# Exact two-valued one-hot rows in a clustered attention with experts: no counts, no masks of q, the row of maxima in the first product

## The chip, the cores and the metric

The program runs on one core of a Trainium2 chip. The metric is device time in microseconds (us) of one execution. The kernel before has a median of 580.08 us over 3 runs (579.9 to 581.32). A profiler recorded one more execution; it took 577.12 us, and the span from its first to its last instruction is 575.0 us.

## The reference

There are 4 batches, 8 heads, 768 positions, head size 64, 16 centroids per head. Each query and each key belongs to the cluster of its nearest centroid (largest cosine). A query attends only to the keys of its own cluster; where its cluster has no keys, every score is equal, and it takes the mean of all values.

```python
mask = q_assign[:, :, :, None] == k_assign[:, :, None, :]
scores = scale * np.matmul(q, k.transpose(0, 1, 3, 2))
scores = np.where(mask, scores, -1000000000.0)
scores = scores - np.max(scores, axis=-1, keepdims=True)
attn = np.exp(scores)
attn = attn / (np.sum(attn, axis=-1, keepdims=True) + 1e-09)
return np.matmul(attn, v).astype(np.float32)
```

The result is 3072 tokens of 512 numbers. A gate picks one of 8 experts for each token, every expert keeps the 80 tokens of highest gate weight, and gives `gate * (max(x @ w1, 0) @ w2)` (1024 hidden units); all other tokens give zero.

## The kernel before

Heads are worked in 16 pairs. Each of q and k is split into a high part (rounded to the short f32 format of one PE pass) and the rest. `KAB` and `QAB` are the six buffers of two planes each: plane 1 holds high and low parts (rows 0 to 63 low k against high q, rows 64 to 127 high k against low q), plane 0 holds the high parts in rows 0 to 63, the one-hot rows of the cluster in rows 64 to 79 and one row more, 80. A score tile is the sum of two products (`scores`, L478 over 128 rows of plane 1, L479 over 81 rows of plane 0); the maxima (`smax`, L441 on PE and L443 on VectorE) take rows 0 to 79 of plane 0. The one-hot row of k is 0 where the key is in the cluster and -1 elsewhere, that of q is 2^100 in its cluster and 0 elsewhere, so that a product over other clusters falls to -2^100. Row 80 is -1 in k, and in q the row of maxima (`shift`), which is so subtracted inside the product. ScalarE then takes the exponential (L484), GpSimd sums the probabilities (L493), PE multiplies with the values (`av`, L502, four matmuls in a group, 96 groups).

`assign` finds the clusters of a pair: similarities (L213), a transpose (L221), equality with the maximum on VectorE (L225, L227), transposes back (L231), a product that resolves ties (L237). For queries whose cluster has no keys it counts: the largest value of each row (L243), a flag (L244), a one-column product (L246) that brings the flag to the rows of q, a factor (L249), and the one-hot rows of q times that factor (L251). A product of these rows with a constant (L300) gives a mask, and VectorE multiplies q with it (L302), so that such a query has q = 0 and no one-hot row, and all its scores are 0. `pair` splits and copies the tensors (L268, L273, L282, L307, copies at L82); `first` and `beside` do the same for the first pair.

The order of all this is not written out. Each part yields steps with an engine, an assumed duration, needs and a due time; a planner (`Flow`) plays the steps through with these numbers and writes the instructions to each engine's queue in the order that results. The due times and some holds are in the table `CFG`. Where PE would be idle at the start, it adds products of ones (L1459). Queues run in order; SP issues nearly all copies. Behind the attention come the gate, the choice of 80 tokens for each expert (a chain of small steps), and the experts, whose weights are converted on ScalarE and VectorE.

Of the kernel before, what the change touches and what calls it, by code (L numbers as in the profile page):

```python
# [7 lines left out]
F32 = mybir.dt.float32  # L8
F32R = mybir.dt.float32r
# [10 lines left out]
CFG = dict(at=dict(sum=-3.87, av=6.53, xT=13.56, lt=4.68, turn=2.79, sm=0.38, exp=-3.44, mx=-2.09), stick=0.98,  # L20
           wait=0.04, idle=0.25, dummy=128, bias=0.22, side=(-1.31, -0.22), prep=(-0.75, 0.12), lead=(-39.19, -31.86,
           -37.55, -36.75, -19.29), zero=(-15.19, 0.47, -13.33, 0.15), start=dict(pe=6.1, act=4.8, dve=7.5, pool=2.5,
           dma=0.0), warm=48, cold=38.0, lag=1.3, hold=dict(dve=(0.2, -0.02), act=(0.42, 0.05), pe=(0.26, -0.02)),
           nab=6, pps=9, sums=8, xts=4, vs=2, skew=3, raws=4, lds=3, keys=1, adds=7, weigh=(8, 5.0, 1.5), slots=(19,
           5), native1=(), native2=(0, 1, 2, 4), early=((2, 6), 185.8), spread=(), mix=dict(ld=-44.02, st=-11.35,
           hi1=3.94, lo1=-19.15, hi2=-1.45, lo2=12.52, xg=-48.58, xp=-11.37, out=18.87, sc=3.79, a0=16, a1=14, a2=10,
           spare=-0.17, half=15, reserve=10, eager=10))
# [14 lines left out]
class Program:  # L42
# [41 lines left out]
    def setup(self):  # L84
# [12 lines left out]
        self.twos, self.id4096 = (K16[:, i * P + NT:(i + 1) * P + NT] for i in (3, 4))  # L97
        self.digit = [K16[0:E, 5 * P + NT + i * E:5 * P + NT + (i + 1) * E] for i in range(4)]
# [5 lines left out]
        self.ident, self.hsel = view["ident"], view["hsel"]  # L104
# [6 lines left out]
        self.sel = con.tile([P, NP, P], F32R, name="sel")  # L111
# [91 lines left out]
    def assign(self, b, p):  # L203
# [32 lines left out]
        fi = self.misc([P, 512])  # L236
        nc.tensor.matmul(fi[:, 0:HS], lhsT=self.tie, rhs=es, start=True, stop=True)  # L237
        yield Step("act", .58, also=("dve", .95), needs=[("ohq", *divmod(r - 2, self.NP))] if r > 2 else [])
        oh = st["oh", b, p] = w.tile([P, HS], F32R, name="oh", bufs=2)
        nc.scalar.activation(oh[0:64], fi[0:64, 0:HS], AF.Identity, bias=self.negone[0:64])  # L240
        z = w.tile([P, 1], F32, name="z", bufs=2)
        z16 = w.tile([P, 1], F16, name="zh", bufs=2)
        nc.vector.tensor_reduce(z[0:64], fi[0:64, 0:HS], axis=AX.X, op=ALU.max)  # L243
        nc.vector.tensor_scalar(z16[0:64], z[0:64], 0.5, None, op0=ALU.is_gt)  # L244
        yield Step("pe", .1)
        nc.tensor.matmul(fi[:, HS:HS + 1], lhsT=self.twos[0:64], rhs=z16[0:64], start=True, stop=True)  # L246
        yield Step("dve", .15)
        ne = w.tile([P, 1], F32, name="ne", bufs=2)
        nc.vector.tensor_scalar(ne, fi[:, HS:HS + 1], 0.5, BIG, op0=ALU.is_gt, op1=ALU.mult)  # L249
        yield Step("act", .58, give="misc", key=("oh", b, p))  # L250
        nc.scalar.activation(oh[64:P], fi[64:P, 0:HS], AF.Relu, scale=ne[64:P])  # L251

    def pair(self, b, p):
# [32 lines left out]
        yield Step("none", 0.0, key=("full", "k", b, p), dma=[CP] * 2)  # L286
        for i, g in enumerate(pos):
            copy(self.KAB[g][0:D, 1, :], lo[i * D:(i + 1) * D, :])
        yield Step("none", 0.0, needs=[("oh", b, p)], key=("hi", "k", b, p), late=CFG["lag"], dma=[OH] * 4)
        onehot("k", self.KAB)  # L290
        yield Step("none", 0.0, needs=[("ld", "q", b, p), ("oh", b, p)], key=("ohq", b, p), late=CFG["lag"], dma=[OH] * 4)
        onehot("q", self.QAB)
# [15 lines left out]
        yield Step("none", 0.0, key=("full", "q", b, p), dma=[CP] * 4)  # L308
        for i, g in enumerate(pos):
            copy(self.QAB[g][0:D, 1, :], hi[i * D:(i + 1) * D, :])  # L310
# [9 lines left out]
    def first(self):  # L320
# [37 lines left out]
        fk, cnt, fq = one([P, HS], "st1"), one([P, 1], "st2"), self.spare([P, HS])  # L358
# [25 lines left out]
        for f in range(2):  # L384
            nc.tensor.matmul(mask[f], lhsT=self.sel[:, 2 + f, :], rhs=oh, start=True, stop=True)
# [1388 lines left out]
```

## Time and profile before

| | us |
|---|---|
| median of 3 runs | 580.08 (579.9 to 581.32) |
| profiled execution | 577.12 |
| its span | 575.0 |
| PE busy in the span | 550.9 |
| VectorE busy | 436.6 |
| GpSimd busy | 377.9 |
| ScalarE busy | 375.4 |

The page gives the busy time of each engine and the granted clock of PE over 40 slices. The views used below are the table of windows (busy time in a stretch), the timeline (instructions in order of time), the lines (instructions grouped by line of the kernel) and the waits. PE is the matmul engine, PEld its weight loads, DVE VectorE, ACT ScalarE, POOL GpSimd, SPq the queue of SyncE. An f32 matmul of the values is recorded twice.

### The profile page before, as it was taken

The page shows a single profiled execution, that of the slowest core. Times are in us where ns is not written, and L with a number is a line of the kernel's source. Part 1 is how long each engine was busy: PE and PEld are TensorE (multiplying, and loading weights), DVE is VectorE, ACT ScalarE, POOL GpSimd, SP SyncE. Part 2 cuts the span into 40 slices and gives each one's busy share as a digit, 9 for nine tenths or more (in the row PEclk, how much of TensorE's full clock was granted, in tenths as well). Part 3 has the DMA queues.
Part 4 walks back from the last instruction along what each step waited for, and adds up shares of the span by engine and source line. Part 5 has one row for each costly group of instructions (what it writes and reads, how often), then busy time and mean ns, then how long its engine had stood idle before and what let it go on. Part 6 is the DMA issues. An engine that isn't in the chain of part 4 may idle for free. (4 is left out here: it accounts for less than half of the span.)

```text
span 575.0 us, 11207 instructions
## 1 busy us (share of the span) xinstructions
PE 550.9 (96%) x3939; PEld 358.6 (62%) x3939; DVE 436.6 (76%) x867; ACT 375.4 (65%) x743; POOL 377.9 (66%) x225
## 2 busy tenths in 40 slices
PE   7899999999999999999999999999999977999996
PEld 6566666566657675656566565666765455766574
DVE  4977677777768787767777786797869467997983
ACT  7747777686748676866676775758655363755661
POOL 6339795977597796939796969397995021434531
PEclk9869999999999999999999999999999978999999
DMA  7385667768566858677559577445655595599931
GB/s 256 86 236 152 177 187 205 182 185 233 131 184 179 245 166 221 177 216 172 151 156 239 160 220 188 113 122 133 202 212 219 200 338 184 172 308 387 388 122 34
DMA packets 69591, 112.67 MB, mean 196 GB/s; under 512 B 11328, under 2 KB 38496, under 8 KB 69536
## 3 DMA queue, kind: packets, MB, share of 16 engines
q1 hardware_dynamic: 68512, 109.32, 65.1%
q0 software_dynamic: 1024, 2.64, 1.5%
q8 instruction: 31, 0.51, 0.4%
q14 instruction: 24, 0.20, 0.1%
HBM read 70.96 MB, written 13.99 MB: 148 GB/s over the span
## 5 line engine op out<-in xcount | busy, mean ns | idle before, releaser
L443 DVE TENSOR_REDUCE mx<-sm 128x1 f32<-128x384 f32 x384 | 202.6, 551 | 50.9 <-PE sm L441 49.0
L493 POOL TENSOR_TENSOR sum<-sum,pp 128x768 f32<-128x768 f32 x121 | 217.7, 1832 | 3.2 <-ACT pp L484 2.8
L484 ACT ACTIVATE pp<-st 128x384 f32<-128x384 f32 x384 | 173.4, 486 | 65.4 <-PE st L479 57.0
L502 PE MATMUL av<-pp,ldv 128*64 128x384 f32 x768 | 144.2, 498 | 0.0
L441 PE MATMUL sm<-KAB,QAB 80*128 80x384 f32 x384 | 139.4, 381 | 1.4 <-DVE mx L443 0.6
L478 PE MATMUL st<-QAB,KAB 128*128 128x384 f32 x384 | 135.7, 353 | 0.0
L479 PE MATMUL st<-QAB,KAB 81*128 81x384 f32 x384 | 130.3, 339 | 0.0
L441 PEld LDWEIGHTS sm<-KAB,QAB 80*128 80x128 f32 x384 | 71.3, 192 | 31.8 <-DVE mx L443 12.0
L493 POOL TENSOR_TENSOR sum<-pp 128x768 f32<-128x768 f32 x32 | 58.4, 1830 | 49.5 <-ACT pp L484 49.5
L502 PEld LDWEIGHTS av<-pp,ldv 128*64 128x64 f32 x768 | 46.9, 136 | 62.8 <-issue 60.5
L478 PEld LDWEIGHTS st<-QAB,KAB 128*128 128x128 f32 x384 | 73.4, 191 | 9.1 <-issue 4.8
L479 PEld LDWEIGHTS st<-QAB,KAB 81*128 81x128 f32 x384 | 73.5, 191 | 0.0
L307 POOL TENSOR_TENSOR ldq<-ldq,hi 128x768 fp32r<-128x768 f32 x15 | 27.3, 1818 | 32.5 <-ACT hi L268 30.2
L972 POOL DMA_INDIRECT xg<-xs,gi x8 | 22.0, 2751 | 38.8 <-PE tp L989 19.0
L1376 DVE TENSOR_REDUCE most<-weigh 128x1 f32<-128x1024 f32 x32 | 38.7, 1209 | 4.7 <-DMA weigh<-in_w_dram 4.7
L282 POOL TENSOR_TENSOR ldk<-ldk,hi 128x768 fp32r<-128x768 f32 x15 | 27.3, 1821 | 7.9 <-issue 7.8
L948 DVE SCALAR_TENSOR_TENSOR w1p<-raw,scales,w1p 128x512 f16<-128x512 f32 (+1 forms) x36 | 29.3, 862 | 2.5 <-ACT w1p L939 2.5
L1022 PEld LDWEIGHTS <-w1p 128*128 128x128 f16 x768 | 28.6, 100 | 3.8 <-issue 3.8
L1022 PE MATMUL hp<-xt,w1p 128*128 128x80 f16 x768 | 29.5, 202 | 0.3 <-DVE xt L1000 0.3
L1081 POOL DMA_INDIRECT out_dram<-room,si x8 | 11.6, 1445 | 26.3 <-ACT room L1074 16.1
L939 ACT ACTIVATE w1p<-raw,scales 128x1024 f16<-128x1024 f32 x22 | 24.0, 1141 | 2.1 <-DMA raw<-in_w_dram 2.1
L273 ACT CAST QAB<-hi 64x768 fp32r<-64x768 f32 x30 | 25.0, 832 | 0.7
(253 smaller groups left out, 687.9 us busy)
## 6 DMA issues: line engine op xcount, KB each, us to landing
raw<-in_w_dram SPq DMA_DIRECT2D x34, 512.0 KB
weigh<-in_w_dram SPq DMA_DIRECT2D x32, 512.0 KB
room<-in_w_dram SPq DMA_DIRECT2D x25, 512.0 KB
ldk<-in_kT_dram SPq DMA_DIRECT2D x16, 384.0 KB
ldq<-in_qT_dram SPq DMA_DIRECT2D x16, 384.0 KB
ldv<-in_v_dram SPq DMA_DIRECT2D x16, 384.0 KB
out_dram<-zero SPq DMA_DIRECT2D x24, 256.0 KB
QAB<-hi SPq DMA_DIRECT2D x31, 192.0 KB
```

The lines of the kernel that those rows point to most:

```text
L282: nc.gpsimd.tensor_tensor(lo, t, hi.bitcast(F32), op=ALU.subtract)
L307: nc.gpsimd.tensor_tensor(lo, t, hi.bitcast(F32), op=ALU.subtract)
L441: nc.tensor.matmul(s, lhsT=qj, rhs=k[0:D + C, 0, f * HS:(f + 1) * HS], start=True, stop=True)
L443: nc.vector.tensor_reduce(mx[:, j, f:f + 1], s, axis=AX.X, op=ALU.max)
L478: nc.tensor.matmul(s, lhsT=k[:, 1, ks], rhs=q[:, 1, qs], start=True, stop=False)
L479: nc.tensor.matmul(s, lhsT=k[0:D + C + 1, 0, ks], rhs=q[0:D + C + 1, 0, qs], start=False, stop=True)
L484: self.nc.scalar.activation(self.st["pp", g, c][:, f], self.st.pop(("s", g, c, f)), AF.Exp, scale=float(self.D) ** -0.5)
L493: eng.tensor_tensor(flat(t), flat(a), flat(self.st["pp", g, c]), op=ALU.add)
L502: nc.tensor.matmul(a[i * D:(i + 1) * D, f, 0:HS], lhsT=v[:, c, i, :], rhs=st["pp", 2 * r + i, c][:, f], start=(c == 0), stop=(c == NC - 1) ...
L948: nc.vector.scalar_tensor_tensor(t[:, 1, fs], raw[:, 0, fs], s, t[:, 0, fs], op0=ALU.mult, op1=ALU.subtract)
L1022: nc.tensor.matmul(hp[:, f, :], lhsT=wt[:, a, fs], rhs=xt[:, x, k, :], start=(k == 0 and i == 0), stop=(k == K - 1 and i == 2))
L1376: nc.vector.tensor_reduce(self.most[:, R + n:R + n + 1], t, axis=AX.X, op=ALU.max, apply_absolute_value=True)
```

## The change

The one-hot rows become exact: `hit` makes 2^100 or 0 for q, `miss` makes 0 or -1 for k. For a query of an empty cluster every score is now q.k - 2^100, which rounds to -2^100, and so does its maximum; the difference is 0 if the maximum is added before -2^100 is. So the row of maxima moves to the first product: it takes row 0 of plane 1, and the row that was there moves to row 80 of plane 0. The counts (L243 to L249), the mask products (L300) and the products of q (L302) are gone. Copies of 64 rows into plane 1 become one of 63 rows and one of a single row. The one-hot rows of k and q are copied in one step of their own (`ohs`). The table `CFG` has new due times, and two steps of `shift` are bound to follow each other.

```diff
-CFG = dict(at=dict(sum=-3.87, av=6.53, xT=13.56, lt=4.68, ...
+CFG = dict(at=dict(sum=-1.08, av=6.7, xT=10.95, lt=4.66, ...
...
-        oh = st["oh", b, p] = w.tile([P, HS], F32R, name="oh", bufs=2)
-        nc.scalar.activation(oh[0:64], fi[0:64, 0:HS], AF.Identity, bias=self.negone[0:64])
-        nc.vector.tensor_reduce(z[0:64], fi[0:64, 0:HS], axis=AX.X, op=ALU.max)
-        nc.vector.tensor_scalar(z16[0:64], z[0:64], 0.5, None, op0=ALU.is_gt)
-        nc.tensor.matmul(fi[:, HS:HS + 1], lhsT=self.twos[0:64], rhs=z16[0:64], start=True, stop=True)
-        nc.vector.tensor_scalar(ne, fi[:, HS:HS + 1], 0.5, BIG, op0=ALU.is_gt, op1=ALU.mult)
-        nc.scalar.activation(oh[64:P], fi[64:P, 0:HS], AF.Relu, scale=ne[64:P])
+        st["oh", b, p] = w.tile([P, HS], F32R, name="oh", bufs=2)
+        self.rows(st["oh", b, p], fi, fi)
+        yield Step("none", 0.0, needs=self.vacated(g0), key=("ohs", b, p), late=CFG["lag"], dma=[OH] * 8)
+        for n, AB in (("k", self.KAB), ("q", self.QAB)):
+            for i in range(2):
+                self.onehot(AB[(g0 + i) % CFG["nab"]], st["oh", b, p], n == "q", i)
+    def hit(self, dst, src):
+        self.nc.scalar.activation(dst, src, AF.Relu, scale=BIG)
+    def miss(self, dst, src):
+        self.nc.vector.tensor_scalar(dst, src, 1.0, -1.0, op0=ALU.is_ge, op1=ALU.add)
+    def rows(self, oh, fk, fq):
+        self.hit(oh[64:P], fq[64:P])
+        self.miss(oh[0:64], fk[0:64])
...
+        def split(AB, src):
+            for i, g in enumerate(pos):
+                copy(AB[g][1:D, 1, :], src[i * D + 1:(i + 1) * D, :])
+                copy(AB[g][D + C:D + C + 1, 0, :], src[i * D:i * D + 1, :])
...
-            nc.tensor.matmul(mask, lhsT=self.sel[:, 2 + f, :], rhs=self.st["oh", b, p], start=True, stop=True)
-            nc.vector.scalar_tensor_tensor(t[:, fs], mask, 1.0 / BIG, t[:, fs], op0=ALU.mult, op1=ALU.mult)
...
-        for i, g in enumerate(pos):
-            copy(self.QAB[g][0:D, 1, :], hi[i * D:(i + 1) * D, :])
+        split(self.QAB, hi)
...
+        def const(AB, key):
+            return [*moved(AB), (Step("pool", .7, key=key), lambda: nc.gpsimd.memset(AB.bitcast(F32)[0:1, 1, :], -1.0))]
...
-        self.copy(q[D + C:D + C + 1, 0, :].rearrange("o (j p) -> o j p", p=P), row)
+        self.copy(q[0:1, 1, :].rearrange("o (j p) -> o j p", p=P), row)
...
-            nc.gpsimd.memset(t.bitcast(F32)[64:96, 0, :], -1.0)
+            nc.gpsimd.memset(t.bitcast(F32)[0:1, 1, :], -1.0)
```

PE's queue while the fourth pair is prepared, before (`sm` maxima, `st` scores, `av` values, `zh` the flags of the count, `sel` the constant of the mask; the numbers behind names are buffers):

```order
L441 MATMUL sm<-KAB_114,QAB_108 128x384
L502 MATMUL av<-pp,ldv 64x384 x4
L300 MATMUL misc<-oh,sel 128x384
L441 MATMUL sm<-KAB_114,QAB_108 128x384 x2
L478 MATMUL st<-QAB_106,KAB_112 128x384
L479 MATMUL st<-QAB_106,KAB_112 128x384
L478 MATMUL st<-QAB_106,KAB_112 128x384
L479 MATMUL st<-QAB_106,KAB_112 128x384
L300 MATMUL misc<-oh,sel 128x384
L478 MATMUL st<-QAB_107,KAB_113 128x384
L479 MATMUL st<-QAB_107,KAB_113 128x384
```

The same place of the program after the change, where the ties product (L236, before L237) is the last product of the assignment (the lines of the scores are now L459 and L460, of the maxima L428):

```order
L460 MATMUL st<-QAB_105,KAB_111 128x384
L236 LDWEIGHTS K_62
L236 MATMUL misc<-es,K_62 128x384
L428 MATMUL sm<-KAB_113,QAB_107 128x384
L459 MATMUL st<-QAB_106,KAB_112 128x384
L460 MATMUL st<-QAB_106,KAB_112 128x384
L428 MATMUL sm<-KAB_113,QAB_107 128x384
L459 MATMUL st<-QAB_106,KAB_112 128x384
L460 MATMUL st<-QAB_106,KAB_112 128x384
L483 MATMUL av<-pp,ldv 64x384 x4
```

The two mask products that stood among scores have no successor, nor has the count ten rows above them.

VectorE's queue at the start, from the one-hot rows of the first head to the second head's maxima, before (`z`, `zh`, `ne` belong to the counts, `mx` are the maxima, `mr` those over all keys):

```order
L243 TENSOR_REDUCE z<-misc 64x1
L244 TENSOR_SCALAR zh<-z 64x1
L388 SCALAR_TENSOR_TENSOR ldq<-st,ldq 128x384 x2
L411 CAST QAB_104<-ldq 64x768
L443 TENSOR_REDUCE mx<-sm 128x1 x4
L249 TENSOR_SCALAR ne<-misc 128x1
L443 TENSOR_REDUCE mx<-sm 128x1 x3
L302 SCALAR_TENSOR_TENSOR ldq<-misc,ldq 128x384
L443 TENSOR_REDUCE mx<-sm 128x1
L302 SCALAR_TENSOR_TENSOR ldq<-misc,ldq 128x384
L457 TENSOR_TENSOR m_472<-mx 128x6
L458 SCALAR_TENSOR_TENSOR mr<-m_472 128x6
```

After (`amx` and `eq` find the clusters, L254 makes the rows of k):

```order
L254 TENSOR_SCALAR KAB_109<-st 16x384 x2
L224 TENSOR_REDUCE amx<-misc 128x24
L226 TENSOR_TENSOR eq<-misc,amx 128x384
L254 TENSOR_SCALAR oh_327<-st 64x384
L430 TENSOR_REDUCE mx<-sm 128x1 x6
L254 TENSOR_SCALAR oh<-misc 64x384
L430 TENSOR_REDUCE mx<-sm 128x1 x6
L439 TENSOR_REDUCE mr<-mx 128x6
L430 TENSOR_REDUCE mx<-sm 128x1 x12
L439 TENSOR_REDUCE mr<-mx 128x6
```

The counts and the four products of q are gone from between the maxima; two one-hot halves are new.

SP's queue with the copies of the third pair, before (`hi` high parts, `ldk` the rest of k, `oh` one-hot rows, `row` the row of maxima):

```order
L82 DMA KAB_114<-ldk 64x768
L82 DMA KAB_115<-ldk 64x768
L82 DMA KAB_114<-oh 16x384 x2
L82 DMA KAB_115<-oh 16x384 x2
L82 DMA QAB_108<-oh 16x384 x2
L82 DMA QAB_109<-oh 16x384 x2
L195 DMA ldk<-in_kT_dram 128x768
L82 DMA QAB_106<-row 1x6x128
```

After:

```order
L82 DMA KAB_113<-oh 16x384 x2
L82 DMA KAB_114<-oh 16x384 x2
L82 DMA QAB_107<-oh 16x384 x2
L82 DMA QAB_108<-oh 16x384 x2
L82 DMA QAB_105<-row 1x6x128
L82 DMA KAB_113<-ldk 63x768
L82 DMA KAB_113<-ldk 1x16x48
L82 DMA KAB_114<-ldk 63x768
L82 DMA KAB_114<-ldk 1x16x48
```

The row of maxima of an earlier head stands among these copies, and each copy of the rest of k is now two.

## Rows read from the trace of the kernel before

**Rows 1.** The page: busy us, share, instructions; clock in tenths over 40 slices.
```profile
PE 550.9 (96%) x3939; PEld 358.6 (62%) x3939; DVE 436.6 (76%) x867; ACT 375.4 (65%) x743; POOL 377.9 (66%) x225
...
PEclk9869999999999999999999999999999978999999
```

**Rows 2.** Windows of the span; columns are named in the first row.
```profile
core 0: us, PE busy (x) PEld busy (x) DVE busy (x) ACT busy (x) POOL busy (x), PEclk, DMA share, GB/s
44.00:450.00 406.00, 401.49 (x2347) 257.69 (x2347) 310.54 (x617) 278.82 (x593) 319.33 (x178) 1.00 0.66 181
450.00:488.00 38.00, 29.62 (x385) 20.85 (x384) 23.46 (x80) 17.99 (x29) 5.92 (x12) 0.87 0.84 269
488.00:565.00 77.00, 75.79 (x952) 51.02 (x953) 69.43 (x85) 47.95 (x64) 29.73 (x12) 1.00 0.74 261
```

**Rows 3.** Timeline of PE: a mask product inside a run (start, duration).
```profile
122.80 0.34 PE L479 MATMUL st<-QAB,KAB 81*128 81x384 f32 x1
122.98 0.34 PE L300 MATMUL misc<-oh,sel 128*128 128x384 f32 x1
123.16 0.33 PE L478 MATMUL st<-QAB,KAB 128*128 128x384 f32 x1
```

**Rows 4.** Lines of PE from 44 to 450 us: busy us, mean ns.
```profile
L300 PE MATMUL misc<-oh,sel 128*128 128x384 f32 x27 | 10.0, 371 | 0.0
...
L246 PE MATMUL misc<-zh,K 64*128 64x1 f16 x13 | 2.1, 163 | 1.6 <-DVE zh L244 1.5
```

**Rows 5.** Timeline of PE: a count inside a run.
```profile
116.20 0.33 PE L441 MATMUL sm<-KAB,QAB 80*128 80x384 f32 x1
116.69 0.16 PE L246 MATMUL misc<-zh,K 64*128 64x1 f16 x1 [0.16 <-DVE zh L244]
116.78 0.44 PE L478 MATMUL st<-QAB,KAB 128*128 128x384 f32 x1
117.06 0.34 PE L479 MATMUL st<-QAB,KAB 81*128 81x384 f32 x1
```

**Rows 6.** Timeline: value groups, alone and two in one run.
```profile
100.75 0.62 PE L441 MATMUL sm<-KAB,QAB 80*128 80x384 f32 x2
101.30 1.51 PE L502 MATMUL av<-pp,ldv 128*64 128x384 f32 x8
102.74 0.55 PE L527 MATMUL misc<-K,xT 128*128 128x128 f32 x3
...
450.78 2.80 PE L502 MATMUL av<-pp,ldv 128*64 128x384 f32 x16
...
453.51 2.79 PE L544 MATMUL sm<-sum,unit 128*32 128x384 f32 x32
```

**Rows 7.** Waits of PE and its loads, 44 to 450 us: us, times, longest.
```profile
PE misc L221 <- ACT row L464: 2.0, 9, 0.3
...
PEld sm L441 <- DVE mx L443: 7.0, 12, 0.7
```

**Rows 8.** The start: timeline of ScalarE, VectorE and PE.
```profile
9.47 1.44 ACT L400 CAST KAB<-ldk 64x384 fp32r<-64x384 f32 x3
...
15.48 0.54 DVE L443 TENSOR_REDUCE mx<-sm 128x1 f32<-128x384 f32 x1
...
30.03 1.16 PE L441 MATMUL sm<-KAB,QAB 80*128 80x384 f32 x2
31.37 1.15 PE L441 MATMUL sm<-KAB,QAB 80*128 80x384 f32 x2
32.09 1.02 DVE L443 TENSOR_REDUCE mx<-sm 128x1 f32<-128x384 f32 x2 [0.31 <-PE sm L441]
32.32 0.52 PE L478 MATMUL st<-QAB,KAB 128*128 128x384 f32 x1
```

**Rows 9.** Copies of L82 on SP: ns min/median/max to issue; who waited.
```profile
L82 SPq DMA_DIRECT2D QAB<-oh x64: 507/587/1315, 18.6 to 399.9; - x64
...
L82 SPq DMA_DIRECT2D QAB<-row x32: 694/762/838, 28.0 to 431.2; - x32
...
  PEld av L502: 0.6, 1
```

**Rows 10.** Lines of GpSimd from 44 to 450 us.
```profile
L493 POOL TENSOR_TENSOR sum<-sum,pp 128x768 f32<-128x768 f32 x120 | 215.9, 1832 | 3.1 <-ACT pp L484 2.8
...
L307 POOL TENSOR_TENSOR ldq<-ldq,hi 128x768 fp32r<-128x768 f32 x14 | 25.5, 1818 | 30.2 <-ACT hi L268 30.2
```

More of the change, by code (lines that the diff above doesn't have):

```diff
@@ L19 @@
 BASE = 0x3C000000
[L20 to L23, printed above, removed]
+CFG = dict(at=dict(sum=-1.08, av=6.7, xT=10.95, lt=4.66, turn=3.4, sm=1.03, exp=-2.62, mx=-2.04), stick=1.27,
+           wait=0.04, idle=0.25, dummy=128, bias=0.7, side=(-1.11, -5.68), prep=(-0.42, 0.68), lead=(-34.38, -43.96,
+           -38.31, -23.0, -20.03), zero=(-4.93, 0.38, -25.66, 3.82), start=dict(pe=6.1, act=4.8, dve=7.5, pool=2.5,
+           dma=0.0), warm=48, cold=38.0, lag=1.3, hold=dict(dve=(20.35, 0.02), act=(0.2, 0.07), pe=(0.29, -0.02)),
            nab=6, pps=9, sums=8, xts=4, vs=2, skew=3, raws=4, lds=3, keys=1, adds=7, weigh=(8, 5.0, 1.5), slots=(19,
-           5), native1=(), native2=(0, 1, 2, 4), early=((2, 6), 185.8), spread=(), mix=dict(ld=-44.02, st=-11.35,
-           hi1=3.94, lo1=-19.15, hi2=-1.45, lo2=12.52, xg=-48.58, xp=-11.37, out=18.87, sc=3.79, a0=16, a1=14, a2=10,
-           spare=-0.17, half=15, reserve=10, eager=10))
+           5), native1=(), native2=(0, 1, 2, 4), early=((2, 6), 185.8), spread=(), mix=dict(ld=-44.0, st=-12.9,
+           hi1=7.87, lo1=-15.2, hi2=-2.03, lo2=10.94, xg=-48.04, xp=-9.64, out=18.87, sc=2.88, a0=18, a1=12, a2=11,
+           spare=-0.17, half=14, reserve=10, eager=8))
 SWITCH = {(0, 1): .01, (1, 0): .01, (0, 2): .108, (1, 2): .108, (2, 0): .16, (2, 1): .196, (0, 0): 0.0, (1, 1): 0.0, (2, 2): 0.0}
@@ L285, in pair @@
         yield from place(self.KAB, hi)
-        yield Step("none", 0.0, key=("full", "k", b, p), dma=[CP] * 2)
-        for i, g in enumerate(pos):
[L288 to L292, printed above, removed]
+        yield Step("none", 0.0, key=("hi", "k", b, p))
+        yield Step("none", 0.0, key=("full", "k", b, p), dma=[CP, OH] * 2)
+        split(self.KAB, lo)
+        yield Step("none", 0.0, needs=[("ld", "q", b, p)])
         t = self.st["q", b, p]
@@ L307, in pair @@
         nc.gpsimd.tensor_tensor(lo, t, hi.bitcast(F32), op=ALU.subtract)
[L308 to L310 removed]
+        yield Step("none", 0.0, key=("full", "q", b, p), dma=[CP, OH] * 2 + [CP] * 2)
+        split(self.QAB, hi)
         for i, g in enumerate(pos):
@@ new lines, in second @@
+        def second():
+            self.copy(Q1[1:D, 1], qh[D + 1:2 * D])
+            self.copy(Q1[D + C:D + C + 1, 0], qh[D:D + 1])
+        yield [*act(K0[lo, 0], k[lo], [("ld", "k", 0, 0)]), *act(Q0[lo, 0], q[lo], [("ld", "q", 0, 0)], "raw0"),
+               *act(K0[up, 1], k[lo], key="k0h"), *act(K1[lo, 0], k[up]), *act(Q1[lo, 0], q[up], (), ("hi", 1)), *act(K1[up, 1], k[up], key="k1h")]
+        yield [rest(K0[lo, 1], k[lo], K0[lo, 0], ["sim0", "raw0"], None), *const(K0, "k0l"),
+               rest(K1[lo, 1], k[up], K1[up, 1], ["k1h"], None), *const(K1, "k1l")]
@@ new lines, in beside @@
+        yield [(Step("dve", .8, needs=[("ld", "q", 0, 0)]), lambda: nc.vector.tensor_copy(Q0[lo, 1], q[lo])),
+               (Step("none", 0.0, dma=[OH], key="q0h"), lambda: self.copy(Q0[D + C:D + C + 1, 0], Q0[0:1, 1])),
+               rest(Q0[up, 1], q[lo], Q0[lo, 1], ["sim0"], "q0l")]
+        yield [(Step("none", 0.0, needs=["oh0"], dma=[OH] * 4, key="oh1"), lambda: (onehot(K1, 0, 1), onehot(Q1, 1, 1))),
+               *act(qh[up], q[up], [("hi", 1)]), (Step("none", 0.0, dma=[CP, OH], key="q1h"), second),
```

95 lines of the change are left out of this document (26 added, 69 removed).

## The prediction

> **What bounds the kernel now.** I read the page first: PE is busy 96% of the span, and its granted clock stands at 9 tenths or more in all but a few slices [rows 1]. The table of windows then splits the span: from 44 to 450 us PE works 401.5 of 406 us at a granted clock of 1.00, while VectorE is busy 310.5, ScalarE 278.8 and GpSimd 319.3 us [rows 2]. That stretch holds the attention of nearly all 16 head pairs, and its end is set by how many products PE has to take and how often it changes from one sort to another. In the 38 us behind it PE has 29.6 us of work (scalar routing steps set the pace), then the experts fill PE again for 77 us [rows 2]. So an instruction that leaves PE between 44 and 450 us is worth its whole slot; one that leaves VectorE or ScalarE there is worth nothing by itself.
>
> Third I read the timeline of PE alone. A busy time there overlaps with its neighbours', so I take costs from start to start. Inside a run of scores and maxima one product of 384 columns takes one slot of 0.175 us: 122.80, 122.98, 123.16 [rows 3].
>
> **The change part by part.** The order lists give counts; between the first and the last score before has 28 mask products (L300) and 14 counts (L246), after none. The 96 value groups (4 matmuls each) stand in 92 separate runs before and in 78 after.
>
> *Mask products.* One inside a run costs the slot between 122.98 and 123.16 [rows 3]. Behind a value group it takes more, but then the next product has the change of sort to pay, so its net is the same. 28 x 0.175 = 4.9 us. The lines view has 27 of them in the window [rows 4]. Their 28 products of q by the mask on VectorE cost nothing by themselves and give nothing.
>
> *Counts.* The count L246 has one column, yet it stops the run: the maxima product before it starts at 116.20 and would be followed at 116.375; the next score starts at 116.78, and that score, taken up cold, holds PE to 117.06, 0.28 instead of 0.175 [rows 5]. That is 0.405 + 0.105 = 0.51 us. In the order 11 of the 14 stand inside a run: 5.6 us. Three stand right behind a value group, where PE changes anyway; I take 0.2 us each (between 0 and 0.51, nearest to the slot of a product): 0.6 us.
>
> *Value groups.* One group (8 records, since an f32 matmul is recorded twice) takes 1.44 us from 101.30 to 102.74; two in one run take 2.73 us from 450.78 to 453.51, so 0.15 less than 2 x 1.44. Two maxima shut in between two groups take 0.55 us (100.75 to 101.30) where 2 x 0.175 = 0.35 would do, so 0.20 more [rows 6]. A run saved is worth up to 0.35 us; some transposes that stood at a group's edge now stand inside a run instead, so I take 0.30: 14 x 0.30 = 4.2 us (bounds 0 and 4.9).
>
> *Transposes of the assignment.* L221 waits on PE for ScalarE, 2.0 us in 9 cases [rows 7]. In the new order 13 of the 14 sets stand behind a value group that covers this wait: 2.0 us.
>
> *Maxima moved.* 30 maxima products stand before the first score, 24 in before: 6 x 0.175 = 1.0 us leaves the long stretch (they are paid in the lead, below).
>
> *Waits on VectorE.* Weight loads for maxima wait 7.0 us for an earlier maximum in that window [rows 7]; most of these hide behind a running group. VectorE loses the q products, the small counts and 30 of its 34 copies out of PSUM, which ScalarE takes (busy 279 of 406, so covered; if that cover went, scores would wait for a PSUM buffer). I take 1.0 us, bounds 0 and 7.
>
> *The lead.* The first maximum of VectorE starts at 15.48 [rows 8]. Now two more casts of 0.48 us (1.44 for three) stand on ScalarE ahead of the one that the one-hot rows need, and VectorE does as much before its first maximum as it did: I take 15.48 + 0.96 + 0.2 for hand-overs, 16.7 (estimate). Then 13 pairs of maxima must pass before the first score. At the granted clock of 0.50 a pair takes 1.34 us (30.03 to 31.37); VectorE alone needs 1.02 of that [rows 8]. With 8 pairs at about 1.1 before the clock falls, 5 at 1.34 and one half more of 0.55 plus two small reductions, the first score comes at 32.8 against 32.32 [rows 8]. Loss 0.5 us, bounds -2 (all pairs at 1.02) and +2 (all at 1.34). GpSimd writes the constant row of k only when the one-row copy has landed; the next pair's difference of k is queued behind it, and needed a pair later.
>
> *Copies.* Row 0 of each split tensor now moves by itself: per pair two copies of k and two of q have 63 rows instead of 64, with four one-row copies beside them; SP has 62 more issues at about 0.59 us, 37 us in all [rows 9]. The copies of a pair start while the pair two before it is scored, so a pair's time (406/16 = 25.4 us) lies between them and their first reader, and I cost them at nothing. The row of maxima is now read by the first of the two products of a score, not the second: 0.175 us earlier, once per head; all of PE's queue stands behind that product, but the row is made four units of work ahead, so it is covered too.
>
> *Tail.* The same matmuls of the experts, four weight conversions shifted between engines; one value group fewer is left behind the last score, which only moves 1.4 us into the long stretch. I cost it at nothing, bounds -2 and +2, as the 77 us are full of PE work [rows 2].
>
> Sum: 4.9 + 5.6 + 0.6 + 4.2 + 2.0 + 1.0 + 1.0 - 0.5 = 18.8 us. The profiled execution has a span of 575.0 and took 577.1 us; it would take 558.3. The runs' median, 580.08, lies 3.0 us above that execution; I keep the difference: **561 us**. What is late next is still PE.
>
> **Rivals.**
> *GpSimd takes over (gain about half).* The 10 sums of a pair at 1.83 us and its two differences are 22 us [rows 10], and a pair of 406/16 = 25.4 us would shrink to 24.2. Where scores run dense, probabilities wait for their sum to free a buffer, and PE waits for them. For it: GpSimd is the busiest of the others, 319.3 us [rows 2]. Against it: it would still be idle for 68 us of a stretch of 387 (406 - 18.8 - 319.3). If it binds, value runs and waits give nothing and the masks and counts alone remain, less 2: about 571 us.
>
> *More than summed.* Each break that I priced at 0.30 or 0.51 also delays a neighbour; if all 7.0 us of the VectorE waits go and the lead gains 2, the time is 580.1 - 18.8 - 6 - 2.5 = 552 us.
>
> *Slower: SP's queue.* SP issues in order, and the row of maxima stands in the same queue as the copies. Its 16-row copies take 0.59 us to issue, the 6-row one 0.76 [rows 9]: the shape matters, and a 63-row copy has no row in this trace. If the four extra copies of a pair and their slower landing hold back the row of maxima, the first product of each of some 30 heads waits. It decides from 18.8/30 = 0.63 us per head; at 1 us the time is 580.1 - 18.8 + 30 = 591 us. Against it: of all the L82 copies only one wait of 0.6 us reached PE before [rows 9].
> The Trainium skill ("DMA: Bandwidth & Descriptors", section "Why a DMA increments its semaphore by 16 and not by 1") speaks against the change here: a copy is spread over the largest number of engines up to 16 that divides its outer dimension, so 63 rows run on 9 engines with 7 rows each, where 64 rows run on 16 with 4. By that rule each of the 60 copies lands later by three rows; the 6-row issue time above agrees that shape counts, no run here shows the rest. The sum stays, since 25 us cover it; only this rival's chance rests on it.
>
> **How the numbers follow.** The sum's own case 0.70 (553 to 569 us); half the gain 0.15 (569 to 575); more than summed 0.08; SP's queue 0.04; no effect, because some wait takes everything back, 0.03. The range of 552 to 570 takes in the first case and the near edges of the two beside it, and leaves out some 0.17. About 0.3% (1.7 us) is what a measurement of this kernel can tell from none: faster 0.93, same 0.03, slower 0.04.
>
> **What would show it.** In the new profile: the window from the first score to the last some 18 us shorter at clock 1.00 and PE still busy all through; no L300 or L246; the first score near 33 us; from the last score to the end about 123 us, 1.4 less than now (450.5 to 575.0); no waits of PE for a copy. Wrong would be: PE idle for GpSimd or ScalarE in the long stretch (first rival), first products of heads waiting for a DMA (third), or a lead that grows by more than 2 us.

## The result and the profile after

The changed kernel takes 566.0 us (median of 4 runs, 564.85 to 567.26) against 580.7 us of the kernel before on the same chip: ratio 0.9745, interval 0.9712 to 0.9778. The forecast was 561 us with a range of 552 to 570; 14.7 us were gained, not 19. The span of the profiled execution is 563.0 us, of before 575.0, so the two spans differ by 12.0 us only. The profiled execution of before (577.1 us) was faster than any of the 43 timed runs of that kernel on record (578.1 at the lowest); that of the changed kernel (565.2 us) lies among its own. So what is compared between the two traces below leans on one fast execution of before.

The page (busy us, share, instructions; clock in tenths over 40 slices), to be read against [rows 1]:

```profile
PE 540.0 (96%) x3897; PEld 353.6 (63%) x3897; DVE 404.3 (72%) x768; ACT 374.0 (66%) x757; POOL 387.4 (69%) x227
...
PEclk9659999999999999999999999999999988999999
```

Then the windows: the stretch from the second pair's first score to the last score, and the time behind the last score, first after the change, then before; to be read against [rows 2]:

```profile
59.00:438.60 379.60, 379.40 (x2248) 244.76 (x2248) 275.01 (x518) 271.43 (x591) 310.56 (x172) 1.00 0.64 193
```
```profile
438.60:563.00 124.40, 108.89 (x1351) 73.92 (x1350) 90.99 (x161) 67.10 (x95) 42.83 (x26) 0.95 0.71 244
```

```profile
56.70:450.50 393.80, 389.29 (x2281) 249.47 (x2281) 301.30 (x598) 270.17 (x575) 306.91 (x172) 1.00 0.66 182
450.50:575.00 124.50, 109.82 (x1355) 74.27 (x1353) 93.71 (x166) 66.75 (x94) 37.47 (x26) 0.95 0.72 246
```

The long stretch is 14 us shorter (393.8 before, 379.8 after, from the second pair's first score to the last, 58.86 to 438.62 after), PE is busy all through it at a granted clock of 1.00, and GpSimd is idle in 69 us of it. Behind the last score nothing changed (124.5 and 124.4). The loss is at the start. The timelines of VectorE and of PE there, to be read against [rows 8]:

```profile
15.82 3.42 DVE L430 TENSOR_REDUCE mx<-sm 128x1 f32<-128x384 f32 x6
19.55 0.55 DVE L254 TENSOR_SCALAR oh<-misc 64x384 fp32r<-64x384 f32 x1 [0.30 <-ACT oh L251]
```

```profile
32.67 1.15 PE L428 MATMUL sm<-KAB,QAB 80*128 80x384 f32 x2
...
34.01 1.16 PE L428 MATMUL sm<-KAB,QAB 80*128 80x384 f32 x2
37.52 0.66 PE L459 MATMUL st<-QAB,KAB 128*128 128x384 f32 x1 [2.35 <-DMA QAB<-row]
```

The first maximum comes at 15.82, nearly as early as before (15.48). After three pairs a one-hot half for the next pair stands in the way (0.30 us of waiting and 0.55 of work). From 20.02 on a pair of maxima takes 1.34 us (32.67 to 34.01), and the first score stands at 37.52 instead of 32.32: 2.35 us of that are a wait for the copy of the row of maxima. The row itself is made by ScalarE at 24.7, and SP's queue shows where its copy was:

```profile
24.70 0.26 ACT L445 CAST row<-misc 6x128 fp32r<-6x128 f32 x1 [3.48 <-PE misc L442]
```

```profile
25.91 2.42 SPq L82 DMA_DIRECT2D KAB<-oh  x4
28.43 2.43 SPq L82 DMA_DIRECT2D QAB<-oh  x4
30.90 2.69 SPq L82 DMA_DIRECT2D QAB<-hi  x4
33.70 1.17 SPq L82 DMA_DIRECT2D QAB<-ldq  x2
34.97 0.76 SPq L82 DMA_DIRECT2D QAB<-row  x1
```

Ten us lie between the row and its copy, filled by 14 copies for the next pair. The granted clock of this start is 0.50 (1.2 of 2.4 GHz) from 18.0 to 41.9, where before it was 0.73 on the mean up to its first score; PE had been idle for 0.62 and 0.24 us up to 15.50 and 16.42, ahead of the fall; in before it had been idle for 0.68 us up to 15.61, and its clock fell at 17.1 too, but rose again at 20.5. What made the difference is not shown. After, then before:

```profile
18.00:41.90 23.90, 21.55 (x74) 12.87 (x74) 15.04 (x30) 6.15 (x13) 6.57 (x5) 0.50 0.45 141
```

```profile
17.00:32.30 15.30, 14.49 (x69) 9.13 (x67) 13.40 (x31) 8.12 (x16) 5.44 (x3) 0.73 0.33 88
```

Where the 14.0 us of the long stretch went is seen from start to start of PE's products, summed by sort (us, number of records; "beyond" is what a score or maximum took above 0.175 us, by what stood behind it):

| second pair's first score to last score | before | after |
|---|---|---|
| mask products | 5.6 (26) | - |
| counts | 1.2 (13) | - |
| scores and maxima | 215.2 (1054) | 209.9 (1052) |
| - beyond, before a count | 3.2 | - |
| - beyond, before the transposes L221 (now L220) | 2.5 | 0.0 |
| - beyond, before a value group | 6.7 (63) | 5.4 (56) |
| - beyond, before a score or maximum | 14.7 | 17.4 |
| value groups | 130.8 | 130.0 |
| all else | 41.0 | 39.9 |

From the first score of all to the last, 17.1 us are saved (418.2 before, 401.1 after); the 3.1 us that the table leaves out lie between the first score and the second pair's first (24.4 before, 21.3 after).

### The profile page after: what moved, and what is told of

Its sections match the earlier page's. It is cut to its first block, busy times and chain, and to the rows that moved or that the text cites. A ratio compares the mean times of both kernels' runs of the same rounds, so it can differ in the third digit from the quotient of the medians.

```text
span 563.0 us, 11170 instructions
## 1 busy us (share of the span) xinstructions
PE 540.0 (96%) x3897; PEld 353.6 (63%) x3897; DVE 404.3 (72%) x768; ACT 374.0 (66%) x757; POOL 387.4 (69%) x227
## 5 line engine op out<-in xcount | busy, mean ns | idle before, releaser
L465 ACT ACTIVATE pp<-st 128x384 f32<-128x384 f32 x384 | 177.0, 491 | 68.9 <-PE st L460 59.2
L428 PE MATMUL sm<-KAB,QAB 80*128 80x384 f32 x384 | 141.9, 392 | 0.4 <-DVE mx L430 0.2
L483 PE MATMUL av<-pp,ldv 128*64 128x384 f32 x768 | 141.1, 496 | 0.0
L459 PE MATMUL st<-QAB,KAB 128*128 128x384 f32 x384 | 137.0, 357 | 2.4 <-DMA QAB<-row 2.4
L460 PE MATMUL st<-QAB,KAB 81*128 81x384 f32 x384 | 130.4, 340 | 0.0
L428 PEld LDWEIGHTS sm<-KAB,QAB 80*128 80x128 f32 x384 | 72.5, 195 | 35.3 <-DVE mx L430 12.5
L483 PEld LDWEIGHTS av<-pp,ldv 128*64 128x64 f32 x768 | 48.2, 136 | 63.3 <-issue 60.1
L474 POOL TENSOR_TENSOR sum<-pp 128x768 f32<-128x768 f32 x32 | 60.5, 1908 | 36.8 <-ACT pp L465 32.7
L459 PEld LDWEIGHTS st<-QAB,KAB 128*128 128x128 f32 x384 | 73.3, 191 | 18.0 <-issue 11.7
L460 PEld LDWEIGHTS st<-QAB,KAB 81*128 81x128 f32 x384 | 73.5, 191 | 0.0
L1062 POOL DMA_INDIRECT out_dram<-room,si x8 | 16.5, 2068 | 29.9 <-ACT room L1055 18.4
L929 DVE SCALAR_TENSOR_TENSOR w1p<-raw,scales,w1p 128x512 f16<-128x512 f32 (+1 forms) x34 | 26.9, 837 | 0.0
L281 ACT CAST KAB<-hi 64x768 fp32r<-64x768 f32 x30 | 24.9, 829 | 0.4
```

The costliest lines, as they stand in the source:

```text
L281: nc.scalar.copy(AB[g][0:D, 0, :], hi[i * D:(i + 1) * D, :])
L428: nc.tensor.matmul(s, lhsT=qj, rhs=k[0:D + C, 0, f * HS:(f + 1) * HS], start=True, stop=True)
L459: nc.tensor.matmul(s, lhsT=k[:, 1, ks], rhs=q[:, 1, qs], start=True, stop=False)
L460: nc.tensor.matmul(s, lhsT=k[0:D + C + 1, 0, ks], rhs=q[0:D + C + 1, 0, qs], start=False, stop=True)
L465: self.nc.scalar.activation(self.st["pp", g, c][:, f], self.st.pop(("s", g, c, f)), AF.Exp, scale=float(self.D) ** -0.5)
L474: eng.tensor_tensor(flat(t), flat(a), flat(self.st["pp", g, c]), op=ALU.add)
```

## The experiments

All times are medians, all ratios to the kernel before on the same chip, with a 95% interval. The experiments ran on three chips, so kernels are compared by their ratios.

**Parts of the change taken out of before.** Three kernels keep the order of before and only leave work out: the mask products and the products of q; the counts; both. What is left out serves the queries of empty clusters.

```diff
-            nc.tensor.matmul(mask, lhsT=self.sel[:, 2 + f, :], rhs=self.st["oh", b, p], start=True, stop=True)
...
-            nc.vector.scalar_tensor_tensor(t[:, fs], mask, 1.0 / BIG, t[:, fs], op0=ALU.mult, op1=ALU.mult)
```
```diff
-        nc.vector.tensor_reduce(z[0:64], fi[0:64, 0:HS], axis=AX.X, op=ALU.max)
-        nc.vector.tensor_scalar(z16[0:64], z[0:64], 0.5, None, op0=ALU.is_gt)
...
-        nc.tensor.matmul(fi[:, HS:HS + 1], lhsT=self.twos[0:64], rhs=z16[0:64], start=True, stop=True)
...
-        nc.vector.tensor_scalar(ne, fi[:, HS:HS + 1], 0.5, BIG, op0=ALU.is_gt, op1=ALU.mult)
+        ne = self.big
```

> The kernel before, in its own order, without the 30 mask products of the steady pairs (L300) and VectorE's products of q by them (L302); so the zeroing of q for queries of empty clusters is left out. Theory of slots: 28 of them stand between the first and the last score, 0.175 us of PE each, and PE is the bound, so 4.9 us less: about 575.8 us, ratio 0.9915. Rival, the time is taken by another wait: no change (0.3% either way).

> The kernel before, in its own order, without the 15 counts (L243, L244, L246, L249); the factor of the one-hot rows is a constant, so the treatment of empty clusters is left out. Theory of slots: a count stops the run, 11 of 14 at 0.51 us and 3 at 0.2: 6.2 us less, about 574.5 us, ratio 0.989. Rival, only its own slot of about 0.09 us counts: 1.3 us less, ratio 0.998.

> The kernel before, in its own order, without the mask products and without the counts (both parts left out as in the two runs beside it). Theory of slots: the two gains add, 11.1 us less: about 569.6 us, ratio 0.981. Rival, GpSimd or VectorE becomes the bound: clearly less than the sum of the two, under 8 us.

Measured: without masks 578.34 us, 0.9961 (0.9941 to 0.9981), a gain of 2.3 us where 4.9 were expected; without counts 575.07, 0.9891 (0.9863 to 0.9918), 6.3 us where 6.2 were expected; without both 572.11, 0.9854 (0.9831 to 0.9878), 8.5 us, which is what the two single gains add up to. The counts' price holds by these times. The masks' 5.6 us of slots are gone from the trace, but at least part of them comes back as waits: in the profiled execution the long stretch is no shorter (394.3 us, before 393.8). Waits of PE's loads from 60 to 450 us without masks (us in total, times, longest):

```profile
PEld sm L438 <- DVE mx L440: 10.3, 18, 1.8
```

Loads of maxima products wait 10.3 us for VectorE instead of 7.0 [rows 7], scores and maxima in a run now exceed their slots by 17.5 us instead of 14.7, and the value groups take 133.1 us instead of 130.8. Of these 5.1 us at most 1.6 are due to 3.4 us at a granted clock of 0.50 (from 224.8), the rest is not. My reading is that the mask product had stood where the next maximum would have waited anyway; no run isolates that.

**Masks put back into the changed kernel.**

```diff
+        if r > 1:
+            old = st["oh", *divmod(r - 1, self.NP)]
+            for f in range(2):
+                nc.tensor.matmul(fi, lhsT=old[:, 0:P], rhs=old, start=True, stop=True)
```

> The changed kernel with two products of 384 columns added beside the ties product of each pair from the third on, 28 in all, that nothing reads (where before had its mask products); the plan is otherwise the changed one. If each product costs its slot of 0.175 us, 4.9 us: 571 us, ratio 0.983. Rival, from the kernel before without its masks (2.3 us for 28): a product beside a change of sort is partly covered, 568 us, ratio 0.978.

Measured: 571.2 us, 0.9862 (0.9817 to 0.9908). PE's timeline at one pair:

```profile
198.13 0.52 PE L239 MATMUL misc<-oh 128*128 128x384 f32 x2
198.49 0.34 PE L240 MATMUL misc<-es,K 128*128 128x384 f16 x1
```

Two products take 0.36 us, and the long stretch is 384.6 us instead of 379.8: 4.8 us more for 26 products in it. By the runs it is more: 0.9862 against the 0.9745 of the changed kernel is 6.8 us, give or take 3. Here each costs at least its slot. So such a product was worth 0.08 us in one order (2.3/28, with the interval 0.04 to 0.12) and 0.18 in the other (4.8/26; by the runs 0.13 to 0.36). Without masks VectorE's products of q go too, which is not so here; and the added products stand beside the ties product, not where the old ones stood.

**Code and due times apart.** One kernel has the changed code with the table of before, another the code of before with the new table.

```diff
-CFG = dict(at=dict(sum=-1.08, av=6.7, xT=10.95, lt=4.66, ...
+CFG = dict(at=dict(sum=-3.87, av=6.53, xT=13.56, lt=4.68, ...
```

> The changed kernel with the due times and holds of the kernel before (the table CFG unchanged). Its order has 85 runs of value groups between the first and the last score, the changed kernel 77, before 91. Theory of the forecast: the masks and counts give 11 us by themselves, the new due times a further 4: about 569.5 us, ratio 0.981. Rival 1: the due times give nothing, then about 566 us, ratio 0.975. Rival 2: the old due times do not fit the new code, then 575 us or more.

> The kernel before with the new due times alone (counts, masks and copies as before). If the new due times are good by themselves, as the changed code's loss without them (ratio 1.016 against 0.975) suggests, the gain is a part of those 23 us: 568 to 574 us, ratio 0.98 to 0.99. Rival: the due times fit one code only, and with the other code they put instructions in places where something waits: no change or slower, 580 to 590 us, ratio 1.00 to 1.015.

Measured: changed code with old due times 589.5 us, 1.0155 (1.012 to 1.0191), slower than before; old code with new due times 610.84, 1.0507 (1.0462 to 1.0552). Both first guesses fell: the first kernel came out as its second rival, the second lies beyond even its rival's range. Waits of PE in the first, over the whole span:

```profile
PE st L459 <- DMA QAB<-row: 6.4, 4, 3.9
...
PE av L483 <- issue: 4.1, 1, 4.1
```

The row of maxima is late four times, 3.9 us of it at the first score. Against the changed kernel's trace the span is 26.3 us longer: 5.8 before the second pair's first score (64.64, not 58.86), 15.1 from there to the last score (394.9, not 379.8) and 5.3 behind it (129.7, not 124.4). In the middle part scores and maxima take 10.9 us more and the value groups 2.0; 4.1 us are one wait of PE, during which the granted clock fell to 0.50 for 6.8 us (445.4 to 452.2). In the second kernel one short wait stands ahead of a long slow stretch. PE's timeline and the windows around it:

```profile
98.06 0.16 PE L246 MATMUL misc<-zh,K 64*128 64x1 f16 x1 [1.19 <-DVE zh L244]
```
```profile
63.20:98.90 35.70, 34.21 (x200) 20.96 (x198) 26.19 (x51) 25.23 (x54) 28.55 (x16) 1.00 0.73 201
98.90:127.00 28.10, 27.52 (x108) 18.72 (x108) 14.29 (x27) 16.04 (x35) 16.57 (x10) 0.70 0.59 177
```

PE waits 1.19 us for the flag of a count, and the clock stands at 0.50 from 98.9 to 116.0; two more such stretches of 10.2 us follow (218.4 and 334.4). The three make some 18.6 of the 27 us by which this kernel's long stretch is longer than before's (420.8, not 393.8); its first score comes at 42.8 instead of 32.3. So the two halves of the change don't add: code +9, table +29, together -15 us (by the ratios).

**The row of maxima on another queue.** In the changed kernel ScalarE, which makes the row, also issues its copy, for the first two heads; in the changed code with old due times, for all heads.

```diff
-        self.copy(q[0:1, 1, :].rearrange("o (j p) -> o j p", p=P), row)
+        to = q[0:1, 1, :].rearrange("o (j p) -> o j p", p=P)
+        if g < 2:
+            nc.scalar.dma_start(to.bitcast(F32), row.bitcast(F32))
+        else:
+            self.copy(to, row)
```

> The changed kernel, with the row-of-maxima copies of the first two heads issued by ScalarE right after it has made the row, not by SP. In the changed kernel SP issues copies without a break from 18.42 us on, the row is ready at 24.96 and its copy is issued at 34.97, and PE waits 2.35 us for it before the first score. Theory, SP's queue holds the row back: the first score at about 35 us instead of 37.5, no such wait, 2 to 2.5 us less, ratio to the kernel before 0.970 where the changed kernel has 0.9745. Rival, the first score is held by the maxima that stand ahead of it on PE and by the clock: no change.

> The changed code with the old due times (589.5 us), but every row-of-maxima copy issued by ScalarE. There PE waits 6.4 us in 4 places for such a copy. Theory, the code's added copies on SP hold the rows back, and this is what the new due times repair: 6 us or more less, about 583, ratio 1.005. Rival, the loss of the old due times lies in the order on PE itself and its clock: 589, ratio 1.015.

Measured: 564.26 us, 0.9703 (0.9672 to 0.9734), beside the kernel without ones (below) the fastest by its median; and 586.05, 1.0105 (1.0061 to 1.0149), between the two expectations. ScalarE's queue and PE in the first:

```profile
24.63 1.52 ACTq L448 DMA_DIRECT2D QAB<-row  x1
```
```profile
33.66 1.16 PE L428 MATMUL sm<-KAB,QAB 80*128 80x384 f32 x2
34.61 0.52 PE L463 MATMUL st<-QAB,KAB 128*128 128x384 f32 x1
```

The wait is gone, the first score comes at 34.61 right behind the last maxima. This shows SP's queue as the cause of the 2.35 us. What that is worth in time is less sure: 0.9703 against 0.9745 is 2.4 us, but the two intervals overlap, and the span of this execution (563.5) is no shorter than the changed kernel's (563.0). In the second kernel the first score comes at 34.7 instead of 38.9, too, yet most of its loss stays (1.0105 against 1.0155, with intervals that overlap): what the old due times cost the new code is not mainly the rows.

**The one-row copies left out** from the fourth pair on (row 80 of plane 0 then keeps what an earlier head left there):

```diff
-                copy(AB[g][D + C:D + C + 1, 0, :], src[i * D:i * D + 1, :])
+                if b == 0 and p < 3:
+                    copy(AB[g][D + C:D + C + 1, 0, :], src[i * D:i * D + 1, :])
```

> The changed kernel without the one-row copies from the fourth pair on (52 issues of SP fewer, some 31 us of SP; the products of dimension 0 of the low parts are then left out or stale). Theory, with the new due times SP's load is hidden: no change, ratio 0.9745 within 0.003. Rival, the load still costs PE: 2 us or more less.

Measured: 566.73 us, 0.9768 (0.9723 to 0.9813), no gain: the rival needed 0.971 or less. In the long stretch SP's extra load is hidden, as the prediction had it. The first three pairs keep their copies here, so this run says nothing of the first head.

**The clock of the start.** One kernel has about twice as many products of ones before the first score, the other (with the rows of two heads on ScalarE) none between the maxima from 20 us on.

```diff
-            d = CFG["dummy"] / 1175
+            d = CFG["dummy"] / (2350 if t < CFG["cold"] else 1175)
```
```diff
-        if n:
+        if n and not 22 < self.free["pe"] < CFG["cold"]:
```

> The changed kernel with about twice as many products of ones before the first scores. In the changed kernel PE's granted clock is 0.50 from 18.0 to 41.9 us, in the kernel before from 17.1 to 20.5 and from 27.3 to 37.5, and at 0.50 a pair of maxima takes 1.34 us. Theory, idle PE lets the clock fall: with more work it stays at 1.00 longer, the first score comes 2 us or more earlier, ratio 0.970. Rival, the added products themselves delay the maxima or the clock falls whatever PE does: no change or slower, ratio 0.9745 to 0.980.

> The changed kernel with the rows of maxima of the first two heads copied from ScalarE's queue, and without the 25 products of ones that stand between the maxima products before the first score. There a pair of maxima takes 1.34 us on PE at a granted clock of 0.50, 0.39 of it for two products of ones, and VectorE waits 0.32 us in each. Without them a pair takes VectorE's 1.02 to 1.05: 11 pairs by 0.29, 3.2 us less before the first score (31.5 instead of 34.6): 561 us, ratio 0.965. Rival: with less work the granted clock stays at 0.50 longer, past 40 us, and the scores of the first pair give the 3 us back: 564 to 566 us, ratio 0.970 to 0.975.

Measured: 568.11 us, 0.9777 (0.9747 to 0.9806), no gain; 564.16, 0.9709 (0.9678 to 0.974), the same as with the ones, in the rival's range but not by its mechanism. With twice the ones (window and PE's timeline):

```profile
18.00:34.30 16.30, 14.33 (x99) 9.01 (x98) 13.93 (x29) 5.44 (x12) 5.74 (x4) 1.00 0.21 63
```
```profile
22.61 0.91 PE L428 MATMUL sm<-KAB,QAB 80*128 80x384 f32 x2
...
23.70 0.91 PE L428 MATMUL sm<-KAB,QAB 80*128 80x384 f32 x2
```
```profile
33.97 1.16 PE L428 MATMUL sm<-KAB,QAB 80*128 80x384 f32 x2
38.94 0.66 PE L459 MATMUL st<-QAB,KAB 128*128 128x384 f32 x1 [3.81 <-DMA QAB<-row]
```

the clock holds at 1.00 up to 34.3, and a pair of maxima takes 1.09 us (22.61 to 23.70). Yet the last pair starts at 33.97, where it was 34.01: the added ones put the first maximum off to 16.99, and PE stands idle for 1.41 us ahead of 31.81, for what is not shown. And the first score is no earlier, since SP's copy is issued at 36.39 instead of 34.97. Without them (PE's timeline and VectorE's):

```profile
26.21 1.15 PE L428 MATMUL sm<-KAB,QAB 80*128 80x384 f32 x2 [0.19 <-DVE mx L430]
27.54 1.15 PE L428 MATMUL sm<-KAB,QAB 80*128 80x384 f32 x2 [0.19 <-DVE mx L430]
```
```profile
26.93 1.02 DVE L430 TENSOR_REDUCE mx<-sm 128x1 f32<-128x384 f32 x2 [0.32 <-PE sm L428]
```

a pair still takes 1.33 us, though each engine is idle in every pair: PE waits for VectorE's maximum, VectorE for the next product. The maxima have two PSUM buffers (L155 of the changed kernel), so each engine waits for the other's turn; at a granted clock of 1.00 the same turn took 1.09. The ones filled a hole. My 1.02 per pair was wrong.

**VectorE loaded again.** Two products of 128x384 on VectorE in each pair.

```diff
...
+        if b or p > 1:
+            for f in range(2):
+                nc.vector.tensor_tensor(self.scratch[:, f * HS:(f + 1) * HS], t[:, f * HS:(f + 1) * HS], t[:, f * HS:(f + 1) * HS], op=ALU.mult)
```

> The changed kernel with two products of 128x384 on VectorE added in each pair from the third on (28 at about 0.5 us, 14 us of VectorE work), that nothing reads; nothing is added on PE. If PE alone sets the time of the long stretch, no change: 566 us, ratio 0.975. Rival: VectorE's maxima come later and the loads of maxima products wait, one wait of 0.3 to 0.5 us for most of them: 572 to 578 us, ratio 0.985 to 0.995; that would also say that a part of the gain of the change came from VectorE's relief.

Measured: 614.63 us, 1.0609 (1.0574 to 1.0645), far past both. VectorE's lines and PE's waits from 60 to 440 us, and the window of the long stretch:

```profile
L304 DVE TENSOR_TENSOR scratch<-ldq 128x384 f32<-128x384 f32 x26 | 39.6, 1562 | 0.0
```
```profile
PE sm L432 <- DVE mx L434: 21.5, 10, 3.5
```
```profile
65.40:487.10 421.70, 398.00 (x2250) 258.15 (x2248) 312.98 (x544) 272.35 (x591) 315.28 (x172) 0.96 0.57 172
```

The load was 40 us, not 14: one product took 1562 ns on the mean, where the product of q that it was to replace took 551 (26 in the same stretch, one operand in PSUM). So this run doesn't tell what 14 us on VectorE are worth; it shows that two operations of 1.6 us ahead of the maxima are not covered. Of the 42 us by which the long stretch is longer some 18 come from the clock: it stood at 0.50 in six stretches, each during or just behind a wait of PE of 1.8 to 3.5 us. Why the products took so long, see the end.

## Why the prediction was right, and which terms were off

The mechanism was right for the long stretch: PE bounds it, what leaves PE shortens it, and the new time is in the range. But two of the prediction's own signs of being wrong came: the lead grew by 5.2 us, more than 2, and a first product waited for a copy. Between the first score and the last 17.1 us were saved (418.2 before, 401.1 after) where about 18 were forecast. That the two are so close is in part luck: value groups and VectorE's waits came out 5.8 us short of their terms, and 3.1 us came from the first pair's scores, where the forecast's prices give about 1.5 (estimate: 2 masks, 1 count and 4 maxima fewer). Lucky too was the step from the profiled execution to the median. The forecast for that execution was 558.3 us and it took 565.2; 2.2 us of this miss went away because the changed kernel's median lies 0.8 us above its execution, not the 3.0 that the prediction kept from before. Only masks and counts were tried by themselves; the other terms are read from the two traces. Term by term:

- *Counts*, 6.2 us forecast: 4.4 in the table (1.2 + 3.2), 6.3 by leaving them out. Right by the runs; the long stretch of the execution without counts is 2.1 us shorter (391.7, not 393.8), so where the rest lies is not shown.
- *Masks*, 4.9: their slots were 5.6, and in the new order two products a pair do cost 4.8. In the old order they were worth 2.3. Masks and counts together gave 8.5 instead of 11.1. The steps that such a product "is worth its whole slot" and that "its net is the same" behind a value group, and with them one price for all places, were the weak ones.
- *Transposes*, 2.0: 2.5. Right.
- *Maxima moved*, 1.0: 354 maxima stand between the first score and the last, 360 before. Right in number.
- *Value groups*, 4.2: 2.1 (0.8 in the groups, 1.3 before them). The number of runs was read from the order and is right (13 fewer in the long stretch); that a saved edge is worth 0.30 was not measured, and half of it is nearer.
- *VectorE's waits*, a gain of 1.0: a loss of 2.7 inside runs. The loads wait 7.5 us for VectorE now, 7.0 before; taking VectorE's work away freed nothing. That a maxima product waits for its turn of the two PSUM buffers, whatever else VectorE does, would explain it; in the long stretch this is not shown.
- *The lead*, a loss of 0.5 with bounds of -2 and +2: 5.2 at the first score. Here a step failed, that of the copies: "the row is made four units of work ahead, so it is covered". For the first head there is no work ahead of it, and 14 copies stood before its own in SP's queue. That is the slower rival's own mechanism, at one head instead of thirty: a wait of 2.35 us, gone when the copy moves to another queue. The other 2.8 lie among the maxima: from 20.02 to 33.40 ten pairs took 1.34 us each where five were forecast, and a one-hot half with its wait stands between them (0.8 us up to 20.02) that the term left out; PE takes up two more pairs ahead of the score (32.67 and 34.01) where the term had one half; the first maximum, 0.9 earlier than forecast, gives some back. (Its sum 16.7 + 8 x 1.1 + 5 x 1.34 + 0.55 with two reductions of 0.17 is 33.1, not 32.8.) The clock alone is not the reason: in the kernel without masks, whose start is that of before but for two mask products and where it stood at 0.50 from 16.6 to 40.5, the first score came at 32.99.
- *Tail*: 124.4 instead of about 123. The value group saved behind the last score bought nothing.

On the copies of the long stretch the prediction held: PE's products wait for none there. SP's issues of 63 rows and of one row (QAB<-hi and KAB<-ldk now), to be read against [rows 9], with who waited for a copy of L82:

```profile
L82 SPq DMA_DIRECT2D QAB<-hi x62: 516/718/1399, 24.5 to 399.8; - x62
L82 SPq DMA_DIRECT2D KAB<-ldk x60: 515/730/1198, 21.5 to 390.6; - x60
...
  PE st L459: 2.4, 1
```

Each of the two lines mixes both shapes, half and half, so its median is of neither. Taken apart, a copy of 63 rows takes 0.75 us (hi) and 0.78 (ldk) to issue at the median, where one of 64 rows took 0.55 and 0.59 before, and the copy of one row 0.55 and 0.53. The 122 issues together hold SP for 80.9 us, the 61 of before for 36.3: 45 us more, where 37 were forecast, and still only the first head felt it. By the DMA packets in the traces the second 63-row copy of k of a pair has landed 2.6 to 3.0 us after its issue began (ten pairs in which no other copy of that row size was near), a 64-row one 2.4 to 3.4 us (five pairs): it lands no later, and the 25 us cover either.

What the two halves are worth singly was not forecast, and could not have been from the trace: the forecast rested on the order that the planner had made, and that order was read. The 6.3 us beyond masks and counts (14.8 by the ratio, less 8.5) belong to code and table together; no run takes them apart. What in the changed code costs 9 us under the old table is open: some 3 us may be the rows (the intervals overlap), the rest was only located, as above. Open too is whether all rows on ScalarE's queue would gain more under the new table: in the profiled execution of the kernel without ones (570.1 us, 6 more than its median) a row on SP was 2.0 us late once in the middle.

## What to carry to other kernels

Price an instruction in the order that it will stand in: a product of 384 columns was worth 0.08 us in one order and 0.18 in another. A copy's cover has to be looked for at the first use of each queue, not in the steady state: issue the transfer that the first consumer waits for from the engine that makes its data (here the wait of 2.35 us went; the gain in time lay within the noise). A table of due times belongs to the code that it was found with; judge code and table together, since each alone was slower here.

## What the runs showed of the hardware

A short wait of PE in a full stretch can cost more than itself. In the kernel without ones PE waited 2.02 us for a row at 297.2, and the granted clock fell (PE's timeline, then windows):

```profile
297.20 0.69 PE L463 MATMUL st<-QAB,KAB 128*128 128x384 f32 x1 [2.02 <-DMA QAB<-row]
297.68 0.52 PE L464 MATMUL st<-QAB,KAB 81*128 81x384 f32 x1
298.00 0.52 PE L463 MATMUL st<-QAB,KAB 128*128 128x384 f32 x1
```
```profile
290.00:297.10 7.10, 5.17 (x33) 2.76 (x31) 5.24 (x9) 2.77 (x7) 7.10 (x5) 1.00 0.75 226
297.10:303.90 6.80, 6.70 (x22) 4.28 (x23) 1.13 (x3) 2.88 (x6) 2.07 (x2) 0.50 0.70 197
```

For 6.8 us at 0.50 (1.2 of 2.4 GHz) a product of 384 columns takes 0.32 us (297.68 to 298.00) instead of 0.175. The old code under the new table showed the same behind 1.19 us, and twice behind three waits of 0.47 or 0.48, 0.27 and 0.30 us close together (215.9 to 217.1, ahead of 218.4; 331.9 to 333.1, ahead of 334.4). The kernel without masks had 3.4 us at 0.50 from 224.8, behind waits of 1.10 and 0.62 us:

```profile
222.91 0.44 PE L438 MATMUL sm<-KAB,QAB 80*128 80x384 f32 x1 [1.10 <-DVE mx L440]
223.97 0.34 PE L231 MATMUL misc<-K,eq 128*128 128x128 f16 x3 [0.62 <-DVE eq L227]
```

The length of one wait doesn't decide it: a wait of 1.45 us up to 148.37 in the changed code under the old table brought no fall, nor did waits of 2.34 and 2.66 us in the kernel with VectorE loaded (the second up to 372.80):

```profile
113.09 0.44 PE L432 MATMUL sm<-KAB,QAB 80*128 80x384 f32 x1 [2.34 <-DVE mx L434]
```

What decides it was not tried.

An elementwise product on VectorE with both operands in SBUF takes far longer beside GpSimd's sums. Of the 28 added ones the 7 that met no GpSimd instruction took 0.54 to 0.55 us; the other 21 took 0.6 to 3.6, 1.9 on the mean. One pair of each kind, and GpSimd beside the second:

```profile
163.57 1.01 DVE L304 TENSOR_TENSOR scratch<-ldq 128x384 f32<-128x384 f32 x2
...
254.49 4.04 DVE L304 TENSOR_TENSOR scratch<-ldq 128x384 f32<-128x384 f32 x2
```
```profile
254.17 3.94 POOL L478 TENSOR_TENSOR sum<-sum,pp 128x768 f32<-128x768 f32 x2
```

The Trainium skill ("SBUF — State Buffer", section "SBUF: two separate sides") says that VectorE with two SBUF inputs and GpSimd share a pair of ports, and that one of them waits for the other's whole instruction. The trace agrees: each of the two products ends 0.42 us after a sum of GpSimd does (the second at 258.5, which is 254.49 + 4.04, the sum at 258.1). The products of q that the change removes had one operand in PSUM and took 551 ns beside the same GpSimd.
